# Chunk 0 of attention and MLP on one core: four h tiles started over half of x, and w_in's first piece in four parts

## The chip, the core and the metric

One core of a Trainium2 chip runs one kernel. The metric is the time of a whole execution in microseconds (us), the median of the runs shown; lower is better. Before the change it is 256.67 us, median of 3 runs (256.66 to 257.04).

The core has five engines, each with its own list of instructions, which it works off in order. PE (TensorE) multiplies matrices and writes to the PSUM banks. DVE (VectorE), ACT (ScalarE) and POOL (GpSimd) work on elements; POOL takes nothing from PSUM in this kernel. SP (SyncE) issues nearly all DMA transfers. An instruction starts when those ahead of it on its engine have started their turn and the semaphores that it waits for have been raised.

## The reference

```python
# q, k, v: 8 batches x 8 heads x 576 positions x 64
q_s = softmax(q, axis=-1)
k_s = softmax(k, axis=2)                        # over positions
kv  = einsum('bhsd,bhse->bhde', k_s, v)
x   = einsum('bhsd,bhde->bhse', q_s, kv)        # to 4608 tokens x 512
h   = x @ w_in                                  # 512 x 2048
out = gelu_exact(h) @ w_out                     # 2048 x 512
```

(The softmaxes also subtract the maximum and add 1e-9 to the sum.)

## The kernel before, in words

**Tiling.** The tokens go through the second half in nine chunks of 512: chunks 0 to 7 are the first 512 positions of each batch, chunk 8 is what is left of all batches. The 8 heads are 4 head pairs (hp 0 to 3), and a head pair is also one of the four 128-row parts (dm 0 to 3) of the 512 rows of w_in. w_in is kept in bf16 in `wi_bf`, w_out in `wo_bf`. h has 16 tiles of 128 columns (t 0 to 15), each the sum of four matmuls, one for each dm (`h_mm`, L377).

**Stages of a chunk.** Exponentials on ACT (`exp_q`, `exp_k`); sums and scaling of q (`norm_q`: DVE L263, L264; `q_scale` L269 on POOL or DVE); transposes of q on PE into PSUM in two halves of two head pairs (`tp_mm`, L287), and their evacuation into `qT` (`tp_evac`, L296 on DVE, L298 on ACT); casts of v to bf16 (`cast_v`, L188 on ACT, L190 otherwise); kv on PE in 64x64 matmuls, two head pairs a half (`kv_mm`, L225); its division by the sums, to `kvc` (`kv_norm`, DVE L236 and L238); x on PE, two head pairs a half (`x_mm`, L343), and its evacuation into `xT` (`x_evac`, DVE L368, ACT L370); then h and gelu (L383 on ACT), and y against w_out (L637 in chunk 0). Chunk 0 is multiplied in the plain way; later chunks use a seven-product scheme with weight sums (`quad_weights`, `mix_wo`, `h_waves`, `y_phase`), whose first sums DVE prepares while chunk 0 runs.

**Order.** Nothing reorders: each engine's list is the order in which the program is written (`tc.manual_schedule()`). The part that the change touches is written out by hand from L902 to L1028. In chunk 0 of the kernel before, PE's list is: seven warm-up products (L899), both transpose halves, kv of pairs 0 and 1, kv of pairs 2 and 3, x of pairs 0 and 1, x of pairs 2 and 3, then h by `h_phase` in groups of tiles (2, then single ones, 4, 4, single ones), going over dm outside and over the group's tiles inside. So h begins when the x of all head pairs has been issued.

**Loads.** SP issues, in this order: q and k of batch 0 (one part of k goes by ACT's queue), v of batch 0 in four parts, w_in in five pieces (256, 256, 512, 512 and 512 columns; one, one, four, two and two transfers), three of the four pieces of w_out, then q, k, v of batch 1 with the last piece of w_out among them, then batch 2. The pieces land in float32 staging buffers named w0 to w4 (`wst`), and a cast brings them into `wi_bf` or `wo_bf`. A buffer is used again, so a later transfer waits on SP for the cast that reads the earlier content: w_out's pieces 0 to 3 take w0 to w3 behind w_in's. Later the buffers hold the weight sums (w0, w1 and w4) and scratch (w2, w3).

**Casts of w_in.** Piece 0 by POOL, one cast for each dm (`cast_wi_dm`, L848); piece 1 half on POOL and half on DVE (`cast_wi` with "pv", L836 and L837); pieces 2 to 4 on DVE between the gelus' program lines, one cast for each dm (L840).

**PSUM banks.** Eight. `psum_h` hands out banks 0, 1, 2 in turn, `psum_y` 3 and 4, `psum_a` 5; 6 and 7 hold two of kv's tiles in chunk 0.

**Chunk 1's start** (L1005 to L1053) is the other place that the change touches: y of chunk 0 tiles 0 to 13, transposes of chunk 1 in quarters (L307, evacuated by L317 on DVE and L319 on ACT), kv of pairs 0 and 1, y tiles 14 and 15, x, kv of pairs 2 and 3, and then four h matmuls, x of pairs 2 and 3, and the rest of h. v of batch 1 is cast by POOL, one pair after the other.

Of the kernel before, what the change touches and what calls it, by code (L numbers as in the profile page):

```python
# [8 lines left out]
FP32 = mybir.dt.float32  # L9
BF16 = mybir.dt.bfloat16  # L10
# [6 lines left out]
def kernel(  # L17
# [16 lines left out]
    nc = tc.nc  # L34
    B, H, S, D = q.shape
    NT, DM = out.shape
# [29 lines left out]
    def bank(i, name="ps", shape=(128, 512)):  # L66
        return psum.tile(list(shape), FP32, tag=f"k{i}", name=name)
# [116 lines left out]
    def cast_v(b, hp, eng=nc.vector):  # L184
        o = v_aug[b % 2][:, hp, :, 0:D]
        i = st[b]["vf"][:, hp, :].rearrange("p (n d) -> p n d", n=NS)
        if eng is nc.scalar:
            eng.copy(out=o, in_=i)  # L188
        else:
            eng.tensor_copy(out=o, in_=i)  # L190
# [23 lines left out]
    def kv_mm(b, half):  # L214


        if "kv" not in st[b]:
            kv_tiles(b)
        for n in range(NS):
            for i in range(2):  # L220
                for hh in range(2):
                    hp = 2 * half + i
                    pr = slice(hh * 64, hh * 64 + 64)
                    c = slice((hh ^ i) * 64, (hh ^ i) * 64 + 64)
                    nc.tensor.matmul(  # L225
                        st[b]["kv"][hp][c, 0:D + 1], ek[b % 2][pr, hp, n, :],
                        v_aug[b % 2][pr, hp, n, 0:D + 1], start=(n == 0), stop=(n == NS - 1),
                    )

    def kv_norm(b, half=None):  # L230

        if half is not None:
            hps = (2 * half, 2 * half + 1)
            rec = small.tile([128, 2], FP32, tag="reck")
            for i, hp in enumerate(hps):
                nc.vector.reciprocal(rec[:, i:i + 1], st[b]["kv"][hp][:, D:D + 1])  # L236
            for i, hp in enumerate(hps):
                nc.vector.tensor_tensor(  # L238
                    out=kvc[b][:, hp, :], in0=st[b]["kv"][hp][:, 0:D],
                    in1=rec[:, i:i + 1].to_broadcast([128, D]), op=ALU.mult,  # L240
                )
            return
        for i, ps in enumerate(st[b]["kvall"]):
            rec = small.tile([128, 2], FP32, tag="reck")
            nc.vector.reciprocal(rec, ps[:, :, D])
            nc.vector.tensor_tensor(
                out=kvc[b][:, 2 * i:2 * i + 2], in0=ps[:, :, 0:D],
                in1=rec.unsqueeze(2).to_broadcast([128, 2, D]), op=ALU.mult,
            )
# [42 lines left out]

    def tp_evac(b, half, eng="v"):
        o = st[b]["qT"][:, :, 2 * half:2 * half + 2, :]
        if eng == "v":
            nc.vector.tensor_copy(out=o, in_=st[b][f"tp{half}"])  # L296
        else:
            nc.scalar.copy(out=o, in_=st[b][f"tp{half}"])  # L298
# [29 lines left out]
    def x_tile(b, hp, pool, tag):  # L328
        if "xT" not in st[b]:
            st[b]["xT"] = attn_sb.tile([128, HP, M], BF16, tag="xT", name="xT", bufs=1)  # L330
        st[b][f"x{hp}"] = pool.tile([128, M], FP32, tag=tag, name="ps")
# [99 lines left out]

    def quad_weights(w):

        q = quad["s"][w] = wst.tile([128, 4, 2, 512], BF16, tag=("w4", "w1")[w], name="quad_s")
        up, dn = slice(w * 512, w * 512 + 512), slice((w + 2) * 512, (w + 3) * 512)
        a11, a12 = wi_bf[:, 0:2, up], wi_bf[:, 2:4, up]
        a21, a22 = wi_bf[:, 0:2, dn], wi_bf[:, 2:4, dn]
        s1, s2, s3, s4 = (q[:, i] for i in range(4))
        return [
            lambda: tt(s1, a21, a22), lambda: tt(s2, s1, a11, ALU.subtract),  # L440
            lambda: tt(s3, a11, a21, ALU.subtract), lambda: tt(s4, a12, s2, ALU.subtract),
        ]
# [367 lines left out]
                    tt(c11[:, n], c11[:, n], ps[:, n])  # L810
            store(0, j, 0, act_q, sp)

    wi_cols = [256, 256, 512, 512, 512]
    wi_parts = [1, 1, 4, 2, 2]
    wi_off = [0, 256, 512, 1024, 1536]

    def load_wi(i):

        w = wst.tile([128, NDM, 512], FP32, tag=f"w{i}", name="w")
        n = wi_cols[i]  # L820
        src = moe_w_in[:, wi_off[i]:wi_off[i] + n].rearrange("(c p) f -> p c f", p=128)
        d = NDM // wi_parts[i]
        for c in range(0, NDM, d):
            nc.sync.dma_start(out=w[:, c:c + d, 0:n], in_=src[:, c:c + d])
        return w

    def cast_wi(i, w, eng):
        n = wi_cols[i]  # L830
        r = n // 128
        o = wi_bf[:, :, wi_off[i]:wi_off[i] + n].rearrange("p d (c m) -> p d c m", c=r)
        w = w[:, :, 0:n].rearrange("p d (m c) -> p d c m", c=r)
        if eng == "pv":

            nc.gpsimd.tensor_copy(out=o[:, 0:2], in_=w[:, 0:2])  # L836
            nc.vector.tensor_copy(out=o[:, 2:4], in_=w[:, 2:4])  # L837
        else:
            for c in range(NDM):
                nc.vector.tensor_copy(out=o[:, c], in_=w[:, c])  # L840

    def cast_wi_dm(i, w, dm, eng):

        n = wi_cols[i]
        r = n // 128
        o = wi_bf[:, dm, wi_off[i]:wi_off[i] + n].rearrange("p (c m) -> p c m", c=r)
        w = w[:, dm, 0:n].rearrange("p (m c) -> p c m", c=r)
        eng.tensor_copy(out=o, in_=w)  # L848

    def load_wo(i):  # L850
        w = wst.tile([128, 4, DM], FP32, tag=f"w{i}", name="w")
        src = moe_w_out[i * 512:(i + 1) * 512, :]
        if i == 0:
            for h in range(2):
                nc.sync.dma_start(
                    out=w[:, 2 * h:2 * h + 2],
                    in_=src[256 * h:256 * h + 256].rearrange("(p c) f -> p c f", c=2),
                )
            return w
        src = src.rearrange("(p c) f -> p c f", c=4)  # L860
        if i == 3:
            nc.sync.dma_start(out=w[:, 0:2], in_=src[:, 0:2])
            return w
        nc.sync.dma_start(out=w, in_=src)
        return w
# [43 lines left out]
        nc.scalar.dma_start(out=touch[:, i, :], in_=a)  # L909

    load_pair(0, "v", v, 4)
    wi = [load_wi(i) for i in range(5)]
    wo = [load_wo(i) for i in range(3)]
    load_main(1, "q", q, 2)
    load_k1(0)
# [17 lines left out]
    norm_q(0, 0, 2)  # L933
    norm_q(0, 1, 2, nc.vector)
    tp_mm(0, 0)
    cast_v(0, 0, nc.scalar)
    cast_v(0, 1, nc.scalar)
    tp_evac(0, 0)
    cast_v(0, 2, nc.gpsimd)
    cast_v(0, 3, nc.gpsimd)  # L940
    x_tile(0, 0, psum_y, "y")
    x_tile(0, 1, psum_y, "y")
    tp_mm(0, 1)
    tp_evac(0, 1, "s")
    x_tile(0, 2, psum_a, "a")
    kv_mm(0, 0)
    kv_norm(0, 0)
    kv_mm(0, 1)
    kv_norm(0, 1)
    for dm in range(NDM):  # L950
        cast_wi_dm(0, wi[0], dm, nc.gpsimd)
    x_tile(0, 3, psum_h, "h")
    x_mm(0, 0)
    x_evac(0, 0, "s")
    x_evac(0, 1)
    x_mm(0, 1)
    x_evac(0, 2, "s")
    x_evac(0, 3)
    cast_wi(1, wi[1], "pv")
    table(AF.Gelu)  # L960

    def ybank():
        return psum_y.tile([128, M], FP32, tag="y", name="ps")

    sums0 = quad_weights(0)
    h_phase(0, {
        0: [lambda: cast_wi(2, wi[2], "v")],
        2: [lambda: cast_wi(3, wi[3], "v")],
        6: [lambda: cast_wi(4, wi[4], "v")],
        9: sums0[0:2] + [lambda: cast_wo(0, wo[0])],  # L970
        15: [lambda: cast_wo(1, wo[1], eng="s")],
    }, groups={0: 2, 4: 4, 8: 4}, banks={
        3: ybank, 6: ybank, 8: ybank,
        9: lambda: psum_a.tile([128, M], FP32, tag="a", name="ps"),
        10: lambda: bank(6), 11: lambda: bank(7),
    })


    exp_q(1, parts=2)
# [2 lines left out]
    cast_wo(3, wo[3], 1, 1, "s")  # L982
    exp_k(1, parts=2, part=1)
    table(AF.Gelu)
    w16 = wst.tile([128, 2, HK, HN], BF16, tag="w0", name="w16")
    sums = quad_weights(1)
    mix_wo(6, 0)
    for fn in sums0[2:]:
# [6 lines left out]
    yps = [bank(i) for i in (3, 4, 2, 0)]  # L995
    norm_q(1, 0, 2)
    norm_q(1, 1, 2, nc.vector)
    for hp in range(HP):
        cast_v(1, hp, nc.gpsimd)

    def y_part(t, js):
# [11 lines left out]
    kv_mm(1, 0)  # L1013
    tp_quarters_evac(1, tps, 0, "v")
    tp_quarters_evac(1, tps, 1, "s")
    kv_norm(1, 0)
    y_part(14, range(J))
    y_part(15, (0, 1, 2))
# [133 lines left out]
```

## Time and profile before

| what | value |
|---|---|
| median of the runs | 256.67 us |
| profiled execution, whole | 257.07 us |
| its span, first instruction to last | 255.3 us |
| PE busy in the span | 248.8 us (97%) |
| DVE, ACT, POOL busy | 208.1, 188.9, 67.8 us |
| mean granted PE clock | 0.996 of full speed |

By stages of chunk 0, from the view of windows (us):

| window | PE busy | DVE | ACT | POOL | DMA, GB/s |
|---|---|---|---|---|---|
| 0 to 10.60, until the transposes | 9.15 | 4.58 | 6.37 | 2.60 | 302 |
| 10.60 to 14.35, until h | 2.87 | 2.52 | 2.57 | 2.08 | 380 |
| 14.35 to 28.20, h | 13.85 | 12.07 | 9.84 | 1.33 | 413 |
| 28.20 to 44.05, y and the start of chunk 1 | 15.83 | 11.62 | 13.33 | 4.70 | 399 |
| 44.05 to 255.30, the rest | 207.07 | 177.34 | 156.79 | 57.06 | 159 |

How to read the profile: a line of the timeline gives start and duration in us, the engine, the line of the kernel (L190 is line 190), the operation, the tile written and the tiles read, shapes, how many like it were merged, and in brackets how long the engine had been idle and what released it. PEld is PE's loading of weights, which runs beside its matmuls. A matmul's own duration is longer than its distance to the next one, since they are pipelined: distances from start to start are what PE's time is made of. The chain that ended last is followed back from the last instruction to whatever released it.

### The profile page before, as it was taken

How to read it: one execution, taken by the hardware profiler on the slowest of the kernel's cores; microseconds unless marked ns; L12 is line 12 of the kernel's file. 1: busy time of each engine (PE TensorE's matmuls, PEld its weight loads, DVE VectorE, ACT ScalarE, POOL GpSimd, SP SyncE). 2: the span in 40 equal slices, each digit the busy share in tenths (PEclk: the TensorE clock that was granted, in tenths of full speed). 3: DMA queues.
4: the chain of work that ended last, by engine and by line, in shares of the span. 5: the costliest groups of instructions: out<-in, count | busy, mean ns of one | idle time of the engine just before them, and what ended most of it. 6: DMA issues, size and time to landing. Idle time of an engine off the chain costs nothing.

```text
span 255.3 us, 6533 instructions
## 1 busy us (share of the span) xinstructions
PE 248.8 (97%) x2678; PEld 196.1 (77%) x2678; DVE 208.1 (82%) x365; ACT 188.9 (74%) x320; POOL 67.8 (27%) x65
## 2 busy tenths in 40 slices
PE   7999999999999999999999999999999999999993
PEld 3444445448888888888888888888888888888882
DVE  1878796998986989897889788988898889488962
ACT  4875996699977995899589968896886787148720
POOL 1430034000735067006700580058001800040000
PEclk9999999999999999999999999999999999999998
DMA  7999999994449925980499059904920340022024
GB/s 236 396 389 424 403 406 399 400 410 166 62 143 335 265 65 126 328 336 1 114 299 369 7 95 314 374 3 86 270 63 3 82 164 3 0 87 82 1 54 113
DMA packets 43166, 50.23 MB, mean 197 GB/s; under 512 B 20224, under 2 KB 30464, under 8 KB 42880
## 3 DMA queue, kind: packets, MB, share of 16 engines
q1 hardware_dynamic: 42496, 49.19, 58.0%
q10 hardware_dynamic: 640, 0.62, 1.0%
q8 instruction: 21, 0.34, 0.5%
q14 instruction: 9, 0.07, 0.1%
HBM read 36.70 MB, written 9.44 MB: 181 GB/s over the span
## 4 chain that ended last, share of the span: by engine, by line
PE 93%; DMA 4%; POOL 1%; DVE 0%; issue 0%; SPq 0%
PE qa L497 19%; PE ps L377 11%; PE ya L694 10%; PE qb L497 10%; PE yd L694 10%; PE ye L694 6%; PE ps L637 5%; PE yb L694 5%; PE qc L497 5%; PE yx L694 4%; DMA f<-in_v_dram 2%; PE kv L225 2%; PE ps L343 2%; DMA f<-in_q_dram 2%; PE ya L765 1%; PE yd L765 1%
## 5 line engine op out<-in xcount | busy, mean ns | idle before, releaser
L497 PEld LDWEIGHTS <-quad_s 128*128 128x128 bf16 x448 | 43.8, 98 | 5.3 <-issue 0.2
L694 PEld LDWEIGHTS <-g 128*128 128x128 bf16 x448 | 43.3, 98 | 5.8 <-issue 0.4
L269 POOL TENSOR_TENSOR e<-e,recq 128x2048 bf16<-128x2048 bf16 (+1 forms) x9 | 27.4, 3048 | 72.5 <-DVE recq L264 47.4
L694 PEld LDWEIGHTS <-s 128*128 128x128 bf16 x336 | 32.9, 98 | 3.8
L497 PEld LDWEIGHTS <-wi_bf 128*128 128x128 bf16 x336 | 32.8, 98 | 3.9
L497 PE MATMUL qa<-quad_t,quad_s 128*128 128x256 bf16 x224 | 29.3, 272 | 0.0
L377 PE MATMUL ps<-xT,wi_bf 128*128 128x512 bf16 x128 | 28.1, 379 | 0.0
L428 POOL TENSOR_TENSOR y_sb<-y_sb 128x512 f32<-128x512 f32 x14 | 19.5, 1391 | 24.2 <-DVE y_sb L428 21.3
L263 DVE TENSOR_REDUCE qsum<-e 128x16 f32<-128x1024 bf16 (+1 forms) x12 | 20.9, 1742 | 5.0 <-ACT e L173 5.0
L377 PEld LDWEIGHTS <-wi_bf 128*128 128x128 bf16 x128 | 12.3, 97 | 15.2 <-issue 0.8
L428 DVE TENSOR_TENSOR qb<-qa,r 128x512 f32<-128x512 f32 x28 | 18.1, 693 | 5.8 <-ACT g L521 3.1
L505 ACT COPY qc<-qa 128x512 f32<-128x512 f32 x26 | 13.9, 577 | 12.0 <-PE qa L497 11.5
L383 ACT ACTIVATE g<-ps 128x512 bf16<-128x512 f32 x32 | 17.7, 602 | 6.0 <-PE ps L377 5.7
L521 ACT ACTIVATE g<-r 128x512 bf16<-128x512 f32 x28 | 17.3, 633 | 6.2 <-DVE r L428 6.2
L173 ACT ACTIVATE e<-f 128x512 bf16<-128x512 f32 (+1 forms) x42 | 20.5, 559 | 1.5 <-DMA f<-in_q_dram 1.4
L521 ACT ACTIVATE g<-qc 128x512 bf16<-128x512 f32 x28 | 15.2, 595 | 7.6 <-PE qc L497 7.6
L428 DVE TENSOR_TENSOR r<-qa,r 128x512 f32<-128x512 f32 x28 | 18.0, 685 | 0.9 <-PE qa L497 0.7
L190 POOL CAST v_aug<-f 128x576 bf16<-128x576 f32 x26 | 17.7, 713 | 3.9 <-DMA f<-in_v_dram 3.7
L402 DVE TENSOR_TENSOR s<-g 128x1024 bf16<-128x1024 bf16 x28 | 18.6, 684 | 0.0
L178 ACT ACTIVATE ek<-f 128x2304 bf16<-128x2304 f32 (+1 forms) x10 | 17.4, 1738 | 0.6 <-DMA f<-in_k_dram 0.5
L521 ACT ACTIVATE g<-qb 128x512 bf16<-128x512 f32 x28 | 15.1, 595 | 0.7 <-PE qb L497 0.7
L497 PE MATMUL qb<-quad_t,quad_s 128*128 128x256 bf16 x112 | 15.5, 273 | 0.0
(101 smaller groups left out, 468.7 us busy)
## 6 DMA issues: line engine op xcount, KB each, us to landing
out_dram<-y_sb SPq DMA_DIRECT2D x16, 512.0 KB, 3.4
f<-in_k_dram SPq DMA_DIRECT2D x6, 1152.0 KB, 10.2
f<-in_v_dram SPq DMA_DIRECT2D x6, 1152.0 KB, 11.8
f<-in_q_dram SPq DMA_DIRECT2D x6, 1024.0 KB, 8.2
w<-in_moe_w_in_dram SPq DMA_DIRECT2D x6, 512.0 KB, 8.1
f<-in_v_dram SPq DMA_DIRECT2D x8, 288.0 KB, 6.6
f<-in_q_dram SPq DMA_DIRECT2D x4, 512.0 KB, 9.0
w<-in_moe_w_out_dram SPq DMA_DIRECT2D x2, 1024.0 KB, 11.8
```

The costliest lines, as they stand in the source:

```text
L173: nc.scalar.activation(out=dst[:, i], in_=src[:, u], func=AF.Exp)
L178: nc.scalar.activation(out=ek[b % 2][:, i:i + n], in_=st[b]["kf"][:, i:i + n].rearrange("p x (n d) -> p x n d", n=NS), func=AF.Exp,)
L190: eng.tensor_copy(out=o, in_=i)
L263: nc.vector.reduce_sum(out=qsum, in_=st[b]["eq"][:, :, i * w:(i + 1) * w, :], axis=AX.X)
L269: eng.tensor_tensor(out=e, in0=e, in1=st[b]["recq"].unsqueeze(3).to_broadcast([128, J, w, D]), op=ALU.mult,)
L377: nc.tensor.matmul(ps, wi_bf[:, dm, t * 128:(t + 1) * 128], st[c]["xT"][:, dm, :], start=(dm == 0), stop=(dm == NDM - 1),)
L383: nc.scalar.activation(out=st[c]["g"][:, t, :], in_=ps, func=AF.Gelu)
L402: tt(out=s12[:, a, half], in0=g[:, a, half], in1=g[:, b, hi], op=ALU.add)
L428: eng.tensor_tensor(out=out, in0=in0, in1=in1, op=op)
L497: nc.tensor.matmul(held[kind, q][:, u], w, mov[m][:, k], start=(m in (1, 5) and u == 0 and k == 0), stop=(k == 1), skip_group_check=True,)
L521: nc.scalar.activation(out=g[:, t:t + 2, half], in_=held[kind, q], func=AF.Gelu)
L694: nc.tensor.matmul(ps[:, j * HN:(j + 1) * HN], act[m][:, k, j * 128:(j + 1) * 128], wgt[m][:, k, :], start=(first and k == 0 and j == 0), ...
```

## The change

It touches chunk 0 and one cast of chunk 1.

- **Order in chunk 0.** kv of pairs 0 and 1 now comes ahead of the second transpose half, and x of pairs 0 and 1 ahead of kv of pairs 2 and 3. Then come four h matmuls, tiles 0 to 3 over dm 0 alone, into banks 0 to 3; then x of pairs 2 and 3 into banks 5 and 6; then those four tiles over dm 1 to 3, and their gelus. `h_phase` does the other twelve tiles (4, 4 and single ones), in a fixed turn of banks.
- **w_in.** Four pieces of 512 columns in place of five; the first two in four transfers of 256 KB each, one for each dm. All casts are one for each dm: the first piece on POOL, the others on DVE, in one run behind the gelus' program lines.
- **Staging buffers.** w_in takes w0, w2, w3, w4; w_out's pieces w1, w0, w2, w3, so its first piece, now one transfer of 1 MB, takes a buffer that nothing used before. The two weight sums that were in w0 and w1 change places.
- **Engines.** Chunk 0: v of pair 0 is cast by POOL (was ACT), the first half of qT is evacuated by ACT and the second by DVE (the other way round before), x1 and x3 by ACT and x2 by DVE (x1 and x3 were DVE's, x2 ACT's). Chunk 1: v of pair 3 is cast by ACT behind its evacuation of qT (was POOL).

```diff
-    wi_cols = [256, 256, 512, 512, 512]
-    wi_parts = [1, 1, 4, 2, 2]
-    wi_off = [0, 256, 512, 1024, 1536]
+    wi_parts = [4, 4, 2, 2]
...
     def load_wi(i):
-        w = wst.tile([128, NDM, 512], FP32, tag=f"w{i}", name="w")
+        w = wst.tile([128, NDM, 512], FP32, tag=("w0", "w2", "w3", "w4")[i], name="w")
...
+    def cast_wi(i, eng):
+        for dm in range(NDM):
+            eng.tensor_copy(
+                out=wi_bf[:, dm, 512 * i:512 * i + 512].rearrange("p (c m) -> p c m", c=4),
+                in_=wi[i][:, dm].rearrange("p (m c) -> p c m", c=4),
+            )
...
     tp_mm(0, 0)
-    cast_v(0, 0, nc.scalar)
+    cast_v(0, 0, nc.gpsimd)
     cast_v(0, 1, nc.scalar)
-    tp_evac(0, 0)
+    tp_evac(0, 0, "s")
     cast_v(0, 2, nc.gpsimd)
     cast_v(0, 3, nc.gpsimd)
+    cast_wi(0, nc.gpsimd)
     x_tile(0, 0, psum_y, "y")
     x_tile(0, 1, psum_y, "y")
-    tp_mm(0, 1)
-    tp_evac(0, 1, "s")
-    x_tile(0, 2, psum_a, "a")
     kv_mm(0, 0)
     kv_norm(0, 0)
+    tp_mm(0, 1)
+    tp_evac(0, 1)
+    x_mm(0, 0)
+    x_evac(0, 0, "s")
+    x_evac(0, 1, "s")
     kv_mm(0, 1)
     kv_norm(0, 1)
-    for dm in range(NDM):
-        cast_wi_dm(0, wi[0], dm, nc.gpsimd)
-    x_tile(0, 3, psum_h, "h")
-    x_mm(0, 0)
-    x_evac(0, 0, "s")
-    x_evac(0, 1)
+    h_begin(0)
+    hps = [bank(i) for i in range(4)]
+    for t in range(4):
+        h_mm(0, hps[t], t, (0,))
+    x_tile(0, 2, Banks(5), "a")
+    x_tile(0, 3, Banks(6), "a")
     x_mm(0, 1)
-    x_evac(0, 2, "s")
-    x_evac(0, 3)
-    cast_wi(1, wi[1], "pv")
+    x_evac(0, 2)
+    x_evac(0, 3, "s")
     table(AF.Gelu)
...
+    for dm in range(1, NDM):
+        for t in range(4):
+            h_mm(0, hps[t], t, (dm,))
+    for t in range(4):
+        h_gelu(0, hps[t], t)
+    for i in range(1, 4):
+        cast_wi(i, nc.vector)
 
     sums0 = quad_weights(0)
+    turn = (0, 1, 2, 3, 4, 7, 5, 6)
     h_phase(0, {
-        0: [lambda: cast_wi(2, wi[2], "v")],
-        2: [lambda: cast_wi(3, wi[3], "v")],
-        6: [lambda: cast_wi(4, wi[4], "v")],
         9: sums0[0:2] + [lambda: cast_wo(0, wo[0])],
         15: [lambda: cast_wo(1, wo[1], eng="s")],
-    }, groups={0: 2, 4: 4, 8: 4}, banks={
...
-    })
+    }, groups={4: 4, 8: 4}, banks={t: lambda t=t: bank(turn[t % 8]) for t in range(4, NDF)}, t1=4)
...
-    for hp in range(HP):
+    for hp in range(3):
         cast_v(1, hp, nc.gpsimd)
...
     tp_quarters_evac(1, tps, 1, "s")
+    cast_v(1, 3, nc.scalar)
     kv_norm(1, 0)
```

More of the change, by code (lines that the diff above doesn't have):

```diff
@@ L432, in quad_weights @@
     def quad_weights(w):
-        q = quad["s"][w] = wst.tile([128, 4, 2, 512], BF16, tag=("w4", "w1")[w], name="quad_s")
+        q = quad["s"][w] = wst.tile([128, 4, 2, 512], BF16, tag=("w4", "w0")[w], name="quad_s")
         up, dn = slice(w * 512, w * 512 + 512), slice((w + 2) * 512, (w + 3) * 512)
@@ L811, in y_last @@
             store(0, j, 0, act_q, sp)
-    wi_cols = [256, 256, 512, 512, 512]
-    wi_parts = [1, 1, 4, 2, 2]
-    wi_off = [0, 256, 512, 1024, 1536]
+    wi_parts = [4, 4, 2, 2]
     def load_wi(i):
-        w = wst.tile([128, NDM, 512], FP32, tag=f"w{i}", name="w")
-        n = wi_cols[i]
-        src = moe_w_in[:, wi_off[i]:wi_off[i] + n].rearrange("(c p) f -> p c f", p=128)
+        w = wst.tile([128, NDM, 512], FP32, tag=("w0", "w2", "w3", "w4")[i], name="w")
+        src = moe_w_in[:, 512 * i:512 * i + 512].rearrange("(c p) f -> p c f", p=128)
         d = NDM // wi_parts[i]
         for c in range(0, NDM, d):
-            nc.sync.dma_start(out=w[:, c:c + d, 0:n], in_=src[:, c:c + d])
+            nc.sync.dma_start(out=w[:, c:c + d], in_=src[:, c:c + d])
         return w
[L829 to L848, printed above, removed]
+    def cast_wi(i, eng):
[4 more added lines that the diff above has]
+            )
     def load_wo(i):
-        w = wst.tile([128, 4, DM], FP32, tag=f"w{i}", name="w")
+        w = wst.tile([128, 4, DM], FP32, tag=("w1", "w0", "w2", "w3")[i], name="w")
         src = moe_w_out[i * 512:(i + 1) * 512, :]
[L853 to L859, printed above, removed]
         src = src.rearrange("(p c) f -> p c f", c=4)
@@ L911 @@
     load_pair(0, "v", v, 4)
-    wi = [load_wi(i) for i in range(5)]
+    wi = [load_wi(i) for i in range(4)]
     wo = [load_wo(i) for i in range(3)]
@@ L935 @@
     tp_mm(0, 0)
-    cast_v(0, 0, nc.scalar)
+    cast_v(0, 0, nc.gpsimd)
     cast_v(0, 1, nc.scalar)
-    tp_evac(0, 0)
+    tp_evac(0, 0, "s")
     cast_v(0, 2, nc.gpsimd)
     cast_v(0, 3, nc.gpsimd)
+    cast_wi(0, nc.gpsimd)
     x_tile(0, 0, psum_y, "y")
     x_tile(0, 1, psum_y, "y")
-    tp_mm(0, 1)
-    tp_evac(0, 1, "s")
-    x_tile(0, 2, psum_a, "a")
     kv_mm(0, 0)
     kv_norm(0, 0)
+    tp_mm(0, 1)
[3 more added lines that the diff above has]
+    x_evac(0, 1, "s")
     kv_mm(0, 1)
     kv_norm(0, 1)
-    for dm in range(NDM):
-        cast_wi_dm(0, wi[0], dm, nc.gpsimd)
-    x_tile(0, 3, psum_h, "h")
-    x_mm(0, 0)
-    x_evac(0, 0, "s")
-    x_evac(0, 1)
+    h_begin(0)
[4 more added lines that the diff above has]
+    x_tile(0, 3, Banks(6), "a")
     x_mm(0, 1)
-    x_evac(0, 2, "s")
-    x_evac(0, 3)
-    cast_wi(1, wi[1], "pv")
+    x_evac(0, 2)
+    x_evac(0, 3, "s")
     table(AF.Gelu)
-    def ybank():
-        return psum_y.tile([128, M], FP32, tag="y", name="ps")
+    for dm in range(1, NDM):
[5 more added lines that the diff above has]
+        cast_wi(i, nc.vector)
     sums0 = quad_weights(0)
+    turn = (0, 1, 2, 3, 4, 7, 5, 6)
     h_phase(0, {
-        0: [lambda: cast_wi(2, wi[2], "v")],
-        2: [lambda: cast_wi(3, wi[3], "v")],
-        6: [lambda: cast_wi(4, wi[4], "v")],
         9: sums0[0:2] + [lambda: cast_wo(0, wo[0])],
         15: [lambda: cast_wo(1, wo[1], eng="s")],
-    }, groups={0: 2, 4: 4, 8: 4}, banks={
-        3: ybank, 6: ybank, 8: ybank,
-        9: lambda: psum_a.tile([128, M], FP32, tag="a", name="ps"),
-        10: lambda: bank(6), 11: lambda: bank(7),
-    })
+    }, groups={4: 4, 8: 4}, banks={t: lambda t=t: bank(turn[t % 8]) for t in range(4, NDF)}, t1=4)
     exp_q(1, parts=2)
@@ L984 @@
     table(AF.Gelu)
-    w16 = wst.tile([128, 2, HK, HN], BF16, tag="w0", name="w16")
+    w16 = wst.tile([128, 2, HK, HN], BF16, tag="w1", name="w16")
     sums = quad_weights(1)
```

## The prediction

> **What bounds the kernel now.** I read the page's chain that ended last first, then that chain cut to the first 40 us, then the timeline around 10 to 17 us and 40 to 47 us, and last the DMA issues with their times to landing.
>
> ```profile
> PE 93%; DMA 4%; POOL 1%; DVE 0%; issue 0%; SPq 0%
> ```
>
> PE carries the end. What is not PE lies at the start, in this piece of the chain (start, duration in us):
>
> ```profile
> 11.47 0.66 POOL v_aug L190
> ...
> 12.17 0.68 POOL v_aug L190
> ...
> 12.89 0.52 PE kv L225 x34
> 13.42 0.21 DVE rec L236 x2
> 13.63 0.21 DVE kvc L238
> ...
> 13.88 0.54 PE ps L343 x4
> 14.42 13.92 PE ps L377 x64
> 28.34 11.87 PE ps L637 x55
> ```
>
> From the first h matmul on, PE never stops: the timeline puts that matmul at 14.35 and the first y matmul at 28.17, so 64 h matmuls take 13.82 us, 0.216 each, and y follows at the same pace. Before it, PE waits for v of the last head pair, its POOL cast, kv, kv_norm and x. So only two things here can move the time: when h starts, and PE work that comes between its matmuls. The rows from which I rebuild the new start (timeline: start, duration, engine, line):
>
> ```profile
> 10.34 1.23 ACT L188 CAST v_aug<-f 128x576 bf16<-128x576 f32 x2
> ...
> 11.62 0.79 PE L225 MATMUL kv<-v_aug,ek 64*64 64x65 bf16 x38
> ...
> 12.14 0.23 DVE L236 RECIPROCAL rec<-kv 128x1 f32<-128x1 f32 x2 [0.17 <-PE kv L225]
> 12.34 0.36 DVE L238 TENSOR_TENSOR kvc<-kv,rec 128x64 bf16<-128x64 f32 x2
> ...
> 13.18 0.41 PE L343 MATMUL ps<-qT,kvc 64*64 64x512 bf16 x4
> ...
> 13.61 0.59 ACT L370 CAST xT<-ps 128x512 bf16<-128x512 f32 x1 [0.88 <-PE ps L343]
> ...
> 15.02 0.66 POOL L836 CAST wi_bf<-w 128x512 bf16<-128x512 f32 x1
> ```
>
> **Step 1: the first h matmul comes earlier, −0.67 us.** Two chains feed it.
> - Through x. v of pair 1 lands at 10.7 (issued 4.99, 5.7 to landing). ACT has finished exp_k at 10.43 and now casts only this pair: 10.78 to 11.44 (0.66). Engines start some 0.05 after their releaser throughout this trace, so kv of pairs 0 and 1 starts at 11.49 (now 11.62). From there to kvc the rows take 0.52 + 0.56 (11.62 to 12.14 to 12.70): 12.57. The qT half that x needs is evacuated by ACT (11.4 plus 1.01, the duration of L298): 12.44, inside that. x starts at 12.61, its ACT evacuation 0.43 later (13.18 to 13.61), at 13.04, ends 13.63, and h can start at **13.68**.
> - Through w_in. The last v part lands at 12.1 (6.79 + 5.3). Behind it comes the first 256 KB of w_in. The four 256 KB parts of the third piece land at 15.5, 16.1, 16.9 and 17.5, 0.65 apart, so the first lands near 12.77. POOL ends its v casts at 12.84 as now; one cast of 128x512 takes 0.66: 13.54, and at 0.6 apart (L848's four of 128x256 take 1.49, three pitches of 0.36) the others end at 14.1, 14.7 and 15.4. The matmuls want them at 15.0, 15.8 and 16.7: covered by over 0.8. Behind these casts POOL has nothing until 35.51.
>
> kv of pairs 2 and 3 (from 12.89, as now) falls in the hole before 13.68, and so does the second transpose half (0.4 after kv). 14.35 − 13.68 = 0.67. Bounds: 13.55 if the w_in chain alone decided, 13.9 if the first part landed with POOL's present wait (13.60 − 0.35).
>
> **Step 2: x of pairs 2 and 3 now stands among h matmuls, +0.44 us.** Today it ends before h begins. Chunk 1 has the very pattern (four h, four x, h again):
>
> ```profile
> 44.05 1.02 PE L377 MATMUL ps<-xT,wi_bf 128*128 128x512 bf16 x4
> ...
> 45.01 0.41 PE L343 MATMUL ps<-qT,kvc 64*64 64x512 bf16 x4
> ...
> 45.35 1.90 PE L377 MATMUL ps<-xT,wi_bf 128*128 128x512 bf16 x8
> ```
>
> From 44.05 to 45.35 are 1.30; four h matmuls are 0.86; x costs 0.44. Its lower bound is 0.24 (42.96 to 43.20, where kv follows x in the same 64x64 form). After it, the second quarter of h (0.86) covers the evacuation of x2 (DVE, 0.45 after x starts, then 0.68): x starts at 14.64, x2 is there at 15.8, h wants it at 15.84. That is a tie; a stall of up to 0.1 is in the range.
>
> **Step 3: what follows stays covered, 0.** Column group 2 (h tiles 4 to 7) wants its DVE casts at 17.6, 18.4, 19.3, 20.2; they run from 15.8 in pitches of 0.56 (L840) and end by 18.1. Groups 3 and 4 wait for w_in from HBM, whose bytes are unchanged (first halves now at 19.4 and 21.9): casts end near 20.1 to 21.9 and 22.6 to 24.3, wanted from 21.0 and 24.5. The gelus are later (table load after the last x evacuation, 15.7 + 1.28 + 0.2 = 17.2), but their banks are wanted again at 21. Cast counts: POOL does four of 0.66 for four of 0.42 and one of 0.66, DVE loses L837's 0.86; none of it reaches PE. On SP the list has two more w_in issues and one w_out issue less, 0.33 to 0.44 each, while transfers land 6.4 to 8.5 after issue: the queue stays full. The first w_out part now waits for no cast; the second waits for POOL (15.4), the third for DVE's second group (18.0; today's third is issued at 18.15); q, k, v of chunk 1 stand behind them as now.
>
> **Step 4: is the gain still there at chunk 1? 0.** y is 0.23 earlier everywhere. What lands at fixed times there: v pair 3 at 41.8 (34.77 + 7.0), today cast by POOL by 42.48 and used at 43.20. Now ACT casts it behind its 1.01 evacuation: that ends near 41.9, the cast at 42.5; kv wants it at 42.97. ACT's next, the y copy, is due at 42.62. POOL's other three casts and DVE's w_out casts (last end 40.84, wanted at 42.0) have over 0.7. If this cover were gone, at most the 0.23 is lost.
>
> **POOL's v cast beside DVE, 0.** The v cast of pair 0 moves to POOL (10.08 on) beside DVE's L269 (9.64 to 10.91). The nearest row is chunk 1:
>
> ```profile
> 36.77 1.73 DVE L269 TENSOR_TENSOR e<-e,recq 128x1024 bf16<-128x1024 bf16 x1
> ...
> 38.23 0.79 POOL L190 CAST v_aug<-f 128x576 bf16<-128x576 f32 x1 [0.82 <-DMA f<-in_v_dram]
> 39.16 0.67 POOL L190 CAST v_aug<-f 128x576 bf16<-128x576 f32 x1
> ```
>
> The POOL cast beside L269 ended 0.52 after it (38.50 to 39.02); so here it would end at 11.43, no later than ACT's 11.44: 0. [...]
>
> **Sum.** −0.67 + 0.44 = **−0.23 us**. The profiled execution took 257.07 (span 255.3 and 1.77 around it); it would be 256.84. It lies 0.40 above the median of the runs, 256.67, from which the same step gives **256.4**. About 0.2%, or 0.5 us, is what a measurement of this kernel can tell from no change.
>
> **Rivals.**
> - A, faster: x costs 0.24 and h starts at 13.55. 14.35 − 13.55 − 0.24 = 0.56, so 256.1. For it: the w_in chain allows 13.54. Against: the chain through x is made of this trace's own rows, and the change of matmul form is paid in both places at chunk 1. Chance 0.18.
> - B, slower, one mechanism: x of pairs 0 and 1 is held until the second half of qT is evacuated, since both halves are written to one tile and that evacuation is issued ahead of x. DVE does it after kv_norm: 12.62 + 0.69 = 13.31; x at 13.36, its evacuation 13.79 to 14.38, h at 14.43. Then nothing is won at the start and x among h is still paid: 14.43 + 0.44 − 14.35 = +0.52, so 257.2. It decides from where h starts after 13.91 (14.35 − 0.44). For it: the two halves interleave in memory. Against: the halves of e interleave in the same way, and the transposes of half 0 start at 10.63 while DVE writes half 1 until 10.91. Chance 0.17.
> - C: POOL's cast of pair 0 starts only when DVE's L269 ends: 10.91 + 0.67 = 11.58, kv at 11.62 as now, h 0.13 later than forecast: −0.10, so 256.6. For and against: the row above. Chance 0.10.
> - D: chunk 1 takes the gain back (ACT's cast or v's landing is later than Step 4 has it): 256.7. For: these are the only slacks under 0.5. Against: each still has 0.1 to 0.4 left. Chance 0.10.
>
> **Range and chances.** The forecast has 0.45; its own range is 256.2 to 256.6 (start 13.55 to 13.9, tie at x2 lost or not). From A's 256.1 to B's 257.2, with 0.1 below for A's bounds, the range is 256.0 to 257.2. Faster by over 0.2% is most of A and a tail of the forecast, 0.20; slower is B and a little, 0.18; the rest, 0.62, is within.
>
> **What would show it.** In the changed kernel's timeline: first L377 matmul near 13.68, ended by ACT's xT; a break of 0.44 after its fourth; no further idle PE until y, near 27.94. h at 14.4 after an x that waits for DVE's qT copy is B; a kv of chunk 0 at 11.62 released by POOL is C; idle PE before the kv at 43 is D. The forecast is wrong if the first w_in quarter lands much after 12.8, or if x among h costs other than 0.44.

## The result, and the profile after

The median of 13 runs is **257.51 us** (256.97 to 257.79), against 256.81 (256.25 to 257.04) for 13 runs of the kernel before beside them: a ratio of 1.0027, 95% interval 1.0018 to 1.0035. The change costs 0.70 us, where the forecast had a gain of 0.23. The forecast was 256.4, and 257.51 lies above its range.

The profiled execution took 257.78 us, with a span of 255.9 (before: 257.07 and 255.3). Each lies 0.26 to 0.27 above the median of its kernel, so these two traces can be set side by side. The page's chain that ended last looks much as it did:

```profile
PE 93%; DMA 4%; POOL 0%; ACTq 0%; issue 0%; SPq 0%; DVE 0%
```

The same chain cut to the first 40 us (start, duration in us) shows what has taken the place of kv, kv_norm and x:

```profile
6.95 6.32 DMA w<-in_moe_w_in_dram
...
13.32 1.10 POOL wi_bf L828
...
14.47 1.04 PE ps L377 x4
15.50 0.34 PE ps L343 x4
15.84 13.15 PE ps L377 x60
```

h now waits for w_in: the landing of its first quarter at 13.27, then one POOL cast of 1.10. The first h matmul starts at 14.47, not earlier than the 14.35 of before; and the four x matmuls that stood ahead of h now stand inside it. The timeline of that stretch (start, duration, engine, line; in brackets the idle time before and what ended it):

```profile
9.39 1.57 DVE L269 TENSOR_TENSOR e<-e,recq 128x1024 bf16<-128x1024 bf16 x1
...
9.91 2.79 POOL L190 CAST v_aug<-f 128x576 bf16<-128x576 f32 x3
...
11.53 0.48 PE L225 MATMUL kv<-v_aug,ek 64*64 64x65 bf16 x36 [0.54 <-POOL v_aug L190]
...
12.53 0.54 PE L343 MATMUL ps<-qT,kvc 64*64 64x512 bf16 x4
12.60 0.69 DVE L296 COPY qT<-ps 128x1024 bf16<-128x1024 bf16 x1
...
13.11 1.07 ACT L370 CAST xT<-ps 128x512 bf16<-128x512 f32 x2 [0.86 <-PE ps L343]
13.32 4.22 POOL L828 CAST wi_bf<-w 128x512 bf16<-128x512 f32 x4 [0.62 <-DMA w<-in_moe_w_in_dram]
...
14.47 1.04 PE L377 MATMUL ps<-xT,wi_bf 128*128 128x512 bf16 x4 [1.06 <-POOL wi_bf L828]
15.43 0.41 PE L343 MATMUL ps<-qT,kvc 64*64 64x512 bf16 x4
...
15.78 3.51 PE L377 MATMUL ps<-xT,wi_bf 128*128 128x512 bf16 x15
...
16.50 2.60 DVE L828 CAST wi_bf<-w 128x512 bf16<-128x512 f32 x3
```

Three places carry the loss, each compared with the profiled execution of before:
- h starts 0.12 later (14.47 against 14.35).
- From the first h matmul to the fifth are 1.31 (14.47 to 15.78), where four take 0.86: x among h costs 0.45.
- POOL's four casts end at 14.42, 15.45, 16.50 and 17.54. The last is wanted at 17.51; the matmul starts at 17.60, 0.08 late.

This is a sum along PE's line; what each place would be worth alone is left to the experiments. Together 0.65, and y starts 0.66 later (28.83 against 28.17). At chunk 1 h starts at 44.71 against 44.05, again 0.66: nothing is added after chunk 0.

That y's start decides holds for all kernels below. The time of the profiled execution less the start of its first y matmul is 228.90 us for before, 228.95 for after, and 228.79 to 229.08 for the experiments, with one exception (e10, 228.34).

### The profile page after: what moved, and what is told of

The parts are those of the page before. It is cut to its first block, busy times and chain, and to the rows that moved or that the text cites. A ratio compares the mean times of both kernels' runs of the same rounds, so it can differ in the third digit from the quotient of the medians.

```text
span 255.9 us, 6530 instructions
## 1 busy us (share of the span) xinstructions
PE 248.7 (97%) x2678; PEld 196.2 (77%) x2678; DVE 207.8 (81%) x363; ACT 189.0 (74%) x321; POOL 70.6 (28%) x64
## 4 chain that ended last, share of the span: by engine, by line
PE 93%; DMA 4%; POOL 0%; ACTq 0%; issue 0%; SPq 0%; DVE 0%
PE qa L497 19%; PE ps L377 11%; PE ya L694 10%; PE qb L497 10%; PE yd L694 10%; PE ye L694 6%; PE ps L637 5%; PE qc L497 5%; PE yb L694 5%; PE yx L694 4%; DMA w<-in_moe_w_in_dram 2%; DMA touch<-in_moe_w_in_dram 2%; PE kv L225 2%; PE ps L343 2%; PE ya L765 1%; PE yd L765 1%
## 5 line engine op out<-in xcount | busy, mean ns | idle before, releaser
L269 POOL TENSOR_TENSOR e<-e,recq 128x2048 bf16<-128x2048 bf16 (+1 forms) x9 | 27.4, 3048 | 71.5 <-DVE recq L264 46.3
L505 ACT COPY qc<-qa 128x512 f32<-128x512 f32 x26 | 13.9, 577 | 12.0 <-PE qa L497 11.5
L190 POOL CAST v_aug<-f 128x576 bf16<-128x576 f32 x26 | 18.4, 744 | 3.0 <-DMA f<-in_v_dram 2.9
L1065 POOL CAST scr<-g 128x1 f32<-128x1 bf16 x4 | 0.8, 188 | 54.6 <-DVE g L405 54.6
```

What stands on the lines that cost most here:

```text
L269: eng.tensor_tensor(out=e, in0=e, in1=st[b]["recq"].unsqueeze(3).to_broadcast([128, J, w, D]), op=ALU.mult,)
```

## The experiments

Before ran beside each group: median 256.78 us for e1 to e4, 256.81 for e5 to e9, 256.74 for e10 and e11. The ratio stands as recorded for the runs; it is not the quotient of the two medians, which for e2 would be 1.0018. "One run" means a single time, which says less than the trace beside it. The last two columns are of one execution each, which can lie some tenths from its kernel's median: e1's took 257.29, e5's 257.40 and e10's 256.19.

| run | time, us | ratio to before | first quarter lands | h starts | y starts |
|---|---|---|---|---|---|
| before, profiled | 257.07 | 1 | not there | 14.35 | 28.17 |
| after | 257.51 | 1.0027 [1.0018, 1.0035] | 13.27 | 14.47 | 28.83 |
| e1_stride2 | 257.07 | 1.0016 [1.0004, 1.0028] | 13.49 | 14.23 | 28.50 |
| e2_stride1 | 257.25 | 1.0027 [1.0015, 1.0040] | 13.31 | 14.04 | 28.31 |
| e3_rows1k | 257.60 | 1.0044 [1.0030, 1.0057] | 13.07 | 14.34 | 28.70 |
| e4_x_first | 258.14 | 1.0063 [1.0050, 1.0076] | 13.27 | 14.48 | 29.23 |
| e5_early | 257.10 | 1.0014 [1.0006, 1.0023] | not waited for | 13.90 | 28.32 |
| e6_dve_first | 257.10 | 1.0016 [1.0007, 1.0026] | 13.45 | 14.04 | 28.29 |
| e7_before_again | 256.92, one run | | not there | 14.18 | 28.01 |
| e9_dm1_first | 257.25, one run | | 13.40 | 14.13 | 28.40 |
| e10_v0_act | 256.86 | 1.0004 [0.9995, 1.0012] | 13.07 | 13.57 | 27.85 |
| e11_one_mb | 258.47, one run | | 14.43 | 15.15 | 29.42 |

**My theory** after reading the two traces: two things that I had priced wrongly hold h back. POOL's casts read w_in's 512 columns in steps of four elements (16 bytes) and so take 1.09 us each, where casts in steps of two had taken 0.66; and the first quarter lands half a microsecond late. **Rivals**: R, the quarter is late because its rows in memory are 2 KB wide; X, what costs is x among the h matmuls, whatever POOL does.

### e1_stride2 and e2_stride1: shorter steps in POOL's casts

The order of the kernel after is kept. Which column of w_in goes with which row of w_out is free, so the first piece is cast in steps of two, or from neighbouring elements, and the first piece of w_out is loaded to match. The cast in e1:

```diff
     def cast_wi(i, eng):
         for dm in range(NDM):
+            if i == 0:
+                eng.tensor_copy(
+                    out=wi_bf[:, dm, 0:512].rearrange("p (g c m) -> p g c m", g=2, c=2),
+                    in_=wi[i][:, dm].rearrange("p (g m c) -> p g c m", g=2, c=2),
+                )
+                continue
```

and in its place in e2:

```diff
+            if i == 0:
+                eng.tensor_copy(out=wi_bf[:, dm, 0:512], in_=wi[i][:, dm])
+                continue
```

> The changed kernel, but POOL's four casts of w_in's first piece read every second element instead of every fourth (w_out's first piece is loaded in two halves to match). Theory P: in the changed kernel POOL's casts (1.09 us each) and the late first quarter of w_in (13.27) set when the first four h tiles start and how fast they go; the 1.09 comes from the step of four. Then a cast takes about 0.66, the first ends at 13.98, h starts at 14.0 instead of 14.47, the last cast is no longer waited for, y starts near 28.3 instead of 28.83: about 257.0, 0.5 below the changed kernel. Rival N (the casts are slow because of what the other engines do beside them): casts stay at 1.09, 257.5. Rival X (the loss is x among the h matmuls): casts shorter, time still 257.4 or more.

> The changed kernel, but POOL's four casts of w_in's first piece read neighbouring elements (w_out's first piece is loaded in 128-row blocks to match). Theory P with the step as the cause: a cast takes 0.60 to 0.66, as v's of 128x576 does, h starts near 13.95, y near 28.25: about 256.9. Rival N: 1.09, 257.5. Rival X: 257.4 or more. If a step of two costs part of it, this one is faster than the one with a step of two.

The groups of POOL's casts by line (least, median and largest duration in ns, first and last start, shape), of the kernel after:

```profile
L828 POOL CAST wi_bf<-w x4: 1087/1095/1101, 13.3 to 16.4; 128x512 bf16<-128x512 f32 x4
```

of e1:

```profile
L829 POOL CAST wi_bf<-w x4: 636/642/646, 13.5 to 15.5; 128x512 bf16<-128x512 f32 x4
```

and of e2:

```profile
L829 POOL CAST wi_bf<-w x4: 616/616/617, 13.4 to 15.2; 128x512 bf16<-128x512 f32 x4
```

The shape and the types are the same in all three lines; only the step differs, and no view prints it. Steps of four take 1.71 times as long as steps of two, and those 1.04 times as long as neighbours. So the cause of the long casts is shown: the step, and not what the other engines do beside them (rival N of the expectations). The jump lies between steps of two (0.642 us) and steps of four (1.095 us); what in POOL makes it, no run shows.

y starts 0.33 (e1) and 0.52 (e2) earlier than after. The medians are 0.44 and 0.26 lower, but those of after come from another group, and e2's ratio is the same 1.0027 as after's. In their own group the kernel to compare with is e3 below, whose casts still read in steps of four (its first quarter comes in two halves): its ratio, 1.0044 [1.0030, 1.0057], lies clear of e1's [1.0004, 1.0028] and overlaps e2's [1.0015, 1.0040]. e2 missed its forecast of 256.9 by 0.35. The traces have e2 ahead of e1, the medians e1 ahead of e2: which is faster is not shown. Neither comes back to before: with h at 14.04 instead of 14.35, a gain of 0.31, and 0.45 for x among h, e2 is still behind.

### e3_rows1k: the first quarter in narrower rows

```diff
         for c in range(0, NDM, d):
+            if i == 0 and c == 0:
+                for f in (0, 256):
+                    nc.sync.dma_start(out=w[:, 0:1, f:f + 256], in_=src[:, 0:1, f:f + 256])
+                continue
```

> The changed kernel, but w_in's first quarter comes in two transfers of 256 columns (rows of 1 KB) instead of one of 512 (rows of 2 KB). Theory R (the dip of the transfer rate at 11 to 12.5 us belongs to the start of rows of 2 KB): the quarter lands near 12.7 instead of 13.27, the casts (still 1.09) start 0.55 earlier, h at 13.9, y near 28.3: about 257.0. Rival F (it belongs to the first reading of w_in, however wide the rows): lands near 13.3, 257.5.

The two halves together landed 1.22 after v's last part; the one quarter of the kernel after needs 1.30, and the two behind it 0.61 and 0.62. The width of the rows is not the reason: R fell, and the time, 257.60, is near that of its rival F (257.5).

### e4_x_first: x of pairs 2 and 3 again ahead of h

```diff
     kv_norm(0, 1)
-    h_begin(0)
-    hps = [bank(i) for i in range(4)]
-    for t in range(4):
-        h_mm(0, hps[t], t, (0,))
     x_tile(0, 2, Banks(5), "a")
...
     x_evac(0, 3, "s")
+    h_begin(0)
+    hps = [bank(i) for i in range(4)]
+    for t in range(4):
+        h_mm(0, hps[t], t, (0,))
```

> The changed kernel, but x of pairs 2 and 3 stands ahead of all h matmuls on PE, as before the change; loads, casts and all else are those of the change. Theory P: nothing is won, since h is paced by POOL's casts (first ends 14.42, last 17.54) and x of 0.44 lies in their shadow: h starts at 14.5, y at 28.8, 257.5. Rival X: the 0.44 of x among h comes back: 257.07.

It became slower still, 258.14. The timeline, PE, POOL and DVE:

```profile
14.48 3.12 PE L377 MATMUL ps<-xT,wi_bf 128*128 128x512 bf16 x12
17.99 1.25 PE L377 MATMUL ps<-xT,wi_bf 128*128 128x512 bf16 x5 [0.39 <-POOL wi_bf L828]
...
13.32 4.62 POOL L828 CAST wi_bf<-w 128x512 bf16<-128x512 f32 x4 [0.54 <-DMA w<-in_moe_w_in_dram]
...
15.87 3.66 DVE L828 CAST wi_bf<-w 128x512 bf16<-128x512 f32 x4 [0.59 <-DMA w<-in_moe_w_in_dram]
```

The four groups of h start at 14.48, 15.52, 16.56 and 17.99, each within 0.06 of the end of a POOL cast (14.42, 15.46, 16.51, 17.94). PE runs at POOL's pace: x among h lay in its shadow, and taking it out alone wins nothing, so X as the whole cause fell. My own forecast of 257.5 failed too, by 0.6. With x early, DVE reaches its casts at 15.87 instead of 16.50, and POOL's last cast stretches from 1.09 to 1.48 beside them; it ends 0.40 later than in after, and y starts 0.40 later.

### e5_early: h without the wait for w_in's first quarter

On top of e2, the cast for dm 0 reads q data that has long landed. It leaves out the wait for w_in's first quarter, and h is computed without the 128 rows of w_in in it; all else stays.

```diff
             if i == 0:
-                eng.tensor_copy(out=wi_bf[:, dm, 0:512], in_=wi[i][:, dm])
+                early = st[0]["qf"][:, 0:2, :].rearrange("p h f -> p (h f)")
+                eng.tensor_copy(out=wi_bf[:, dm, 0:512], in_=early if dm == 0 else wi[i][:, dm])
```

> As e2 (POOL's casts read neighbouring elements), and the cast of dm 0 takes 512 columns of q that landed long before, in place of w_in's first quarter: it computes h with wrong weights in those 128 rows, and leaves out only the wait for that quarter, which is still loaded. Theory P: with both POOL's step and the late quarter out of the way, the forecast's other steps hold: h starts when ACT's x evacuation ends, near 13.75, x among h costs 0.44, y starts near 28.0 against 28.17 before the change: 256.6, some 0.2 below the kernel before. Rival D: chunk 1 waits for v of batch 1 and gives it back: idle PE near 43, 256.8. Rival X (something else in the new order costs more): y at 28.3 or later, 257.0 or more.

h starts at 13.90, right behind ACT's x evacuation (end 13.85): the chain through x. At its head stands POOL's cast of v, moved there by the change:

```profile
11.68 0.48 PE L225 MATMUL kv<-v_aug,ek 64*64 64x65 bf16 x36 [0.98 <-POOL v_aug L190]
```

ACT's cast of pair 1 was done at 10.89, POOL's of pair 0, beside DVE's L269, only at 11.63. x among h costs 15.20 − 13.90 − 0.86 = 0.44. Yet y starts at 28.32: with h at 13.90, 0.45 earlier than before, 0.01 would be left of it, but PE also stands idle for 0.16 at 25.5, where a last part of w_in lands at 24.27 (23.17 before). And chunk 1 takes more back. Its timeline in e5, ACT and PE:

```profile
42.74 0.67 ACT L188 CAST v_aug<-f 128x576 bf16<-128x576 f32 x1 [0.42 <-DMA f<-in_v_dram]
...
43.35 0.58 PE L225 MATMUL kv<-v_aug,ek 64*64 64x65 bf16 x36
...
43.79 0.59 ACT L370 CAST xT<-ps 128x512 bf16<-128x512 f32 x1
...
44.43 1.02 PE L377 MATMUL ps<-xT,wi_bf 128*128 128x512 bf16 x4 [0.17 <-DVE rec L236]
```

v of pair 3 lands at 42.71, ACT casts it until 43.41, its evacuation of x ends at 44.38 and h follows at 44.43. From y's tile 15 to h are 0.56 here, 0.41 in before and after; the kv before it takes 0.58 instead of 0.51. So 0.23 is given back there: rival D's mechanism is real in this trace. It hangs on when v lands, not on an early chunk 0: e2 and e6 start y at the same time (28.31 and 28.29), v of pair 3 lands there at 42.19 and 42.36, and nothing is given back (h at 44.19 and 44.17). The forecast for this run failed by 0.5 us (256.6 against 257.10), and the run came out at the numbers of its rival X (y at 28.3 or later, 257.0 or more). In the trace, h 0.15 later than forecast and the two places, 0.39, make up that much; but this execution, 257.40, is the slowest of its eleven, so how much of it is in the median is not shown.

### e6_dve_first: the first cast on DVE

```diff
-    cast_wi(0, nc.gpsimd)
+    cast_wi(0, nc.gpsimd, (1, 2, 3))
...
     kv_mm(0, 1)
+    cast_wi(0, nc.vector, (0,))
     kv_norm(0, 1)
```

> As e2, and the cast of dm 0 alone goes to DVE, ahead of its kv_norm of pairs 2 and 3. DVE casts 128x512 neighbouring elements in 0.43 (w_out's rows in chunk 1) against POOL's 0.62: with the quarter landing at 13.3, h starts near 13.85, y near 28.1: 256.7, no more than 0.1 below the kernel before. kv_norm moves to 13.75 to 14.3, x of pairs 2 and 3 wants it at 14.8. Rival X: 257.0 or more.

DVE's cast takes 0.42 (13.50 to 13.92), but h starts at 14.04 as in e2. Its timeline:

```profile
10.17 2.82 POOL L190 CAST v_aug<-f 128x576 bf16<-128x576 f32 x3 [0.17 <-DMA f<-in_v_dram]
...
11.82 0.48 PE L225 MATMUL kv<-v_aug,ek 64*64 64x65 bf16 x36 [1.15 <-POOL v_aug L190]
...
14.04 1.02 PE L377 MATMUL ps<-xT,wi_bf 128*128 128x512 bf16 x4 [0.34 <-DVE rec L236]
```

kv waits for POOL's v cast of pair 0, which stood beside DVE's L269 and ended at 11.77; ACT's own cast was done at 11.54. So the chain through x is 0.23 late, ACT's evacuation of x ends at 13.99, and that is what h waits for (the row names DVE's reciprocal, the last releaser it could pair). Repairing the w_in chain has only brought the next one to light: my forecast of 256.7 failed by 0.4, and the time is that of rival X (257.0 or more).

### e7_before_again: the kernel before, one more run

> The kernel before, a second look: its profiled execution took 257.07, above its median of 256.8. If its start varies, h starts earlier than 14.35 here; if its start is the same, the 0.3 lies elsewhere. No theory of the change depends on it, but the size of the loss against the median does.

h starts at 14.18 and y at 28.01; the profiled execution shown before the change had 14.35 and 28.17. Starts move by 0.17 us from one execution to the next, with the landings of v (POOL's first cast of v begins at 11.28 here, 11.47 there). Differences of that size between two single traces are not read here as effects, unless waits and landings in the two traces account for them.

### e10_v0_act: both moved v casts put back

On top of e6, so that what is left of the change is the new order of h, x and kv, w_in's new pieces and buffers, and the exchange of the evacuations between ACT and DVE:

```diff
-    cast_v(0, 0, nc.gpsimd)
+    cast_v(0, 0, nc.scalar)
...
-    for hp in range(3):
+    for hp in range(HP):
         cast_v(1, hp, nc.gpsimd)
...
-    cast_v(1, 3, nc.scalar)
```

> As e6, and the two moved v casts go back: pair 0 of batch 0 to ACT, pair 3 of batch 1 to POOL. In e6 POOL's cast beside DVE's scaling of q took 1.60 and ended 0.23 after ACT's; without it kv of pairs 0 and 1 starts some 0.2 earlier after v's landing, DVE's scaling is back at 1.27, h starts near 13.8, y near 28.1: 256.7, at best 0.1 below the kernel before, which is the most that the new order can give while x among h costs 0.44. If the collision did not matter: 257.1 as e6.

256.86, a ratio of 1.0004 [0.9995, 1.0012]: no difference from before that these runs can tell. PE's timeline:

```profile
11.17 0.47 PE L225 MATMUL kv<-v_aug,ek 64*64 64x65 bf16 x34 [0.28 <-ACT v_aug L188]
...
13.57 1.04 PE L377 MATMUL ps<-xT,wi_bf 128*128 128x512 bf16 x4 [0.55 <-DVE wi_bf L829]
14.54 0.41 PE L343 MATMUL ps<-qT,kvc 64*64 64x512 bf16 x4
14.88 13.12 PE L377 MATMUL ps<-xT,wi_bf 128*128 128x512 bf16 x60
27.85 0.59 PE L637 MATMUL ps<-wo_bf,g 128*128 128x512 bf16 x2
```

kv starts 0.51 earlier than in e5, where v of pair 1 had landed at the same time (10.24 here, 10.20 there): that is what POOL's v cast cost in e5. Against e6 the trace shows no such gain, since there v itself landed at 10.85. h starts at 13.57, even earlier than forecast, and x among h costs 1.31 − 0.86 = 0.45. y starts 0.16 to 0.32 earlier than in the two traces of before; the medians do not show it. This execution, 256.19, is the lowest of its twelve, and 0.5 of its lead lies after y's start, where nothing but buffers differs from before; I did not trace that.

One part of the forecast failed: it expected DVE's L269 back at 1.27 without POOL's v cast beside it. It took 1.69:

```profile
9.45 1.69 DVE L269 TENSOR_TENSOR e<-e,recq 128x1024 bf16<-128x1024 bf16 x1
```

What goes with its length is POOL's own L269. In e10 that ended at 10.06 and DVE's 1.08 later; in before the distance is 1.08 as well (9.83 to 10.91), in after 1.08 too (9.87 to 10.95). In e6 DVE's begins only when POOL's has ended, and takes 1.23.

### e9_dm1_first and e11_one_mb: what the late quarter hangs on

Both on top of e2. e9 sends the rows of dm 1 ahead of those of dm 0; e11 sends the first piece as one transfer of 1 MB over 512 rows. In e9:

```diff
-        for c in range(0, NDM, d):
+        for c in (1, 0, 2, 3) if i == 0 else range(0, NDM, d):
```

and in e11:

```diff
-    wi_parts = [4, 4, 2, 2]
+    wi_parts = [1, 4, 2, 2]
```

> As e2, but of w_in's first piece the quarter of dm 1 is issued ahead of that of dm 0. Theory F (the dip at 11 to 12.5 us goes with the first transfer of 128 rows of w_in, whichever rows): the quarter of dm 1 lands 1.3 after v's last part, that of dm 0 some 0.63 later, near 13.95, and h starts near 14.6. Rival Z (it goes with rows 0 to 127): dm 1 lands 0.65 after v's last part, dm 0 1.3 later.

> As e2, but w_in's first piece comes in one transfer of 1 MB over all 512 rows. Theory F2 (the dip of the transfer rate goes with a first transfer of only 128 rows of w_in): no dip at 11 to 12.5, it lands 2.6 after v's last part, near 14.6; h then starts only near 15.3, y near 29.6, about 258.3. Rival G (it goes with the beginning of w_in in any transfer of 512 columns): the rate dips at 11 to 12.5 again and it lands near 15.3.

In every kernel whose w_in begins with the quarter of dm 0, that quarter (e3: its two halves together) landed 1.22 to 1.70 after v's last part, and the two behind it 0.58 to 0.67 apart. In e9 the delay is smaller and shared: dm 1 landed 0.85 after v, dm 0 0.87 after that. Neither forecast (1.3 and 0.63, or 0.65 and 1.3) was met, so the delay is tied neither to dm 0's rows alone nor wholly to the first place. The windows show it as a fall in what the DMA engines move (window; busy time and instructions of PE, PEld, DVE, ACT, POOL; clock, DMA share, GB/s). After:

```profile
11.00:11.50 0.50, 0.00 (x0) 0.02 (x1) 0.00 (x0) 0.50 (x2) 0.50 (x2) 1.00 1.03 281
11.50:12.00 0.50, 0.47 (x37) 0.43 (x37) 0.00 (x0) 0.50 (x1) 0.50 (x1) 1.00 0.73 123
12.00:12.50 0.50, 0.50 (x11) 0.39 (x8) 0.45 (x4) 0.25 (x1) 0.50 (x2) 1.00 0.79 242
```

e11:

```profile
11.00:11.50 0.50, 0.00 (x0) 0.00 (x0) 0.10 (x1) 0.50 (x2) 0.50 (x1) 1.00 1.04 402
11.50:12.00 0.50, 0.33 (x36) 0.33 (x35) 0.00 (x0) 0.50 (x1) 0.50 (x2) 1.00 1.03 401
12.00:12.50 0.50, 0.50 (x27) 0.46 (x14) 0.31 (x3) 0.04 (x1) 0.50 (x2) 1.00 1.08 422
14.00:14.50 0.50, 0.00 (x0) 0.00 (x0) 0.15 (x2) 0.32 (x1) 0.02 (x1) 1.00 1.06 274
```

and before:

```profile
14.00:14.50 0.50, 0.50 (x5) 0.22 (x5) 0.50 (x2) 0.24 (x2) 0.50 (x3) 1.00 1.08 295
```

With 1 MB over 512 rows the dip at 11.5 is gone (401 instead of 123). It comes, smaller, at 14 to 14.5 (274), where e11's first quarter of 128 rows begins; before has 295 in that window, where its own first quarter begins, and 383 to 386 from 11 to 12.5. So in these traces a dip goes with the first transfers of 128 rows of w_in. In after's dip the DMA engines are not idle: with a share of 0.73 they move 123 GB/s, where e11's share of 1.03 moves 401, so the single transfers take longer. Why they do, no run settles. Nor is it the only dip: further back in the queue single landings come late as well, at places that change from kernel to kernel (in e5 a quarter of the second piece landed 2.15 after the one ahead of it, at 18.68; in e9 the rate falls again to 238 at 14.5 to 15). e11 itself loses more than it saves, since all of the piece must land (14.43) ahead of the first cast.

## Why the prediction was wrong, step by step

**Step 1, −0.67: it failed, and it is the step that decides.** Of its two chains, the one through x was right: kv at 11.53 (forecast 11.49), x at 12.53 (12.61), its evacuation 13.11 to 13.70 (13.04 to 13.63). The one through w_in had two terms that were too small:
- "so the first lands near 12.77": 13.27, +0.50. I took the pitch of quarters in mid-stream for that of the first one. The first transfers of 128 rows that before's trace shows are those of its third piece, and the rate where they begin, 295 GB/s, was there to be read; their landings (14.90, 15.50) did not show it.
- "one cast of 128x512 takes 0.66": 1.09, +0.43, and so a pitch of 1.04 instead of 0.6. The row I took it from, L836 in before, has the same shape and types, but the code behind it reads pieces of 256 columns in steps of two; the new cast reads 512 columns in steps of four. The rearrangement in the code told this, the profile's line did not.

Together the cast ends 0.88 later than forecast (14.42, not 13.54). The chain through x hid 0.09 of it: h starts 0.79 late. With the late quarter and a cast of 0.66, h would start at 14.03 (13.32 + 0.66 + 0.05), 0.35 late; the longer cast adds 0.44. e2 takes the longer cast away and gets to 14.04; e5 takes both away and gets to 13.90, where POOL's v cast holds it. "Covered by over 0.8", which I wrote of the three later casts, was used up by the pitch: the last came 0.08 late.

**Step 2, +0.44: right.** 0.45 in after, 0.44 in e5, 0.45 in e10. The tie at x2 was not lost.

**Step 3, 0: right for the result, with little left.** DVE's first w_in cast took 1.53 instead of 0.62: it stood beside POOL's last one and ended 0.48 after it, at 18.02, and was wanted at 18.47. In e5 w_in's last part, 1.10 later than before, did cost PE 0.16.

**Step 4, 0: right, in this trace by the late start alone.** v of pair 3 landed at 42.97, 1.2 later than before; ACT's cast ended at 43.67 and kv wanted it at 43.86. The slack was 0.19, in e2 and e6, where v landed earlier, 0.46 and 0.27, and in e5 it was gone. The landing at 41.8, which the forecast took over from before, is the term that moved.

**POOL's v cast beside DVE, 0: the size of the collision was right, the 0 was not.** The cast ended 0.53 after DVE's L269 (row: 0.52), and kv came 0.04 later than forecast. But kv waited for it (11.48) and not for ACT's cast, as forecast, which was done at 11.33: it cost the chain through x 0.15, hidden behind the w_in chain. In e6 it cost 0.23 and in e5 0.74, where ACT's cast was done at 10.89. Had the cast begun only at the end of L269, as rival C has it, it would have ended 0.67 after it, its full length; the trace shows 0.53. DVE's L269 itself took 1.57 instead of 1.27, but that goes with POOL's L269 (see e10).

**The rivals.** A needed h at 13.55: not reached by after. B was false: x of pairs 0 and 1 went out at 12.53, ahead of DVE's copy of the second half of qT at 12.60. C came in part: kv was released by POOL's cast, as C has it, but at 11.53 and not 11.62. D was real in e5 and idle in after. The slower side came about by a mechanism that I had not listed, a w_in chain that ends last. The text did name one sign of it ("if the first w_in quarter lands much after 12.8") and gave it no chance of its own. Its bound for h, 13.9, has the cast begin at 13.25 (13.60 − 0.35), near the 13.32 of after: so the late quarter was almost within its bounds, and the longer cast was in none of them. With 14.42 for the end of the cast, its own sum would have been 256.4 + 0.79 = 257.2, and with the last cast's 0.08 still 257.3.

**What is settled and what is open.** Steps of four in POOL's casts and the late first quarter set when h starts in after, and POOL's casts how it goes on (e1, e2, e4, e5). With both out of the way (e5), POOL's v cast decides, and the kernel is still 0.14% behind. With the casts of v put back as well and the quarter still late (e10), what is left of the change is worth nothing that these runs can tell: the earlier start earns about what x among h costs. Open is why w_in's first transfers of 128 rows move so slowly, and how much of each single trace is in the medians.

## What to carry to other kernels

A duration may be taken from a row of the same shape only when the access pattern in the code is the same: the profile prints shape and type, not the step, and here the step alone was worth a factor of 1.7. When work is moved ahead of a wait, price every chain that then ends in that place, the load and the cast too, from its first transfer and not from the pitch in mid-stream. An operation put among others of another form has a price of its own that the earlier start must first earn back: here 0.45 us of at most 0.67.

## What the runs showed of the hardware that was not expected

- POOL's cast of 128x512 from float32 to bf16: 0.616 us from neighbours, 0.642 in steps of two, 1.095 in steps of four. DVE does the same cast in 0.42 from neighbours (e6) and 0.62 in steps of four when POOL is idle (after).
- POOL and DVE delay each other in plain casts too: DVE's single-input cast 1.53 instead of 0.62 beside POOL's (after), POOL's 1.48 instead of 1.09 beside DVE's (e4). The delayed cast ends behind the other one by its own duration less 0.14, three times over: 0.53 of 0.67 (POOL's v cast), 0.48 of 0.62 (DVE's cast, after), 0.95 of 1.09 (POOL's cast, e4). So all but some 0.14 us of it, an estimate from these three, waits. Why the one waits for the other, no run shows.
- A 256 KB transfer of 128 rows landed 1.22 to 1.70 us after the one ahead of it when it was w_in's first (0.85 in e9, where dm 1 came first), and 0.58 to 0.67 for the two behind it (in e9 0.87 and 0.62); one of 1 MB over 512 rows in the same place moved at 401 to 422 GB/s.
